# Linear attention and SwiGLU on one core: batch 0 in two halves of its heads, and the order of the first loads

## The chip, the cores and the metric

One core of a Trainium2 chip runs the whole program. The metric is the device time of one execution in microseconds (us); smaller is better. Executions of one kernel agree within about 0.4%. All runs quoted are of the state that the measurement calls fast. A ratio is the mean time of one kernel's fast runs over the mean of the other's fast runs of the same rounds, so it is not quite the ratio of the medians that stand beside it. The chip changed between the first measurement and the experiments, and between the three rounds of experiments (e1 to e4; e5 to e8; the last four). So each experiment is compared with the kernel before of its own round, and experiments of different rounds by their ratios.

PE is the matrix engine, ACT the scalar engine, DVE the vector engine, POOL the engine that issues the loads. PSUM is the memory that PE writes its results to, in banks. The granted clock is the share of its full speed that PE was given, as the profile records it.

## The reference, cut to what matters

```python
# q, k, v: (8 batches, 8 heads, 576, 64), float32
phi = lambda x: np.where(x > 0, x, np.exp(x) - 1.0) + 1.0     # = max(x, 0) + min(exp(x), 1)
kv  = einsum('bhsd,bhse->bhde', phi(k), v)                    # "kv", R in the kernel
z   = sum(phi(k), axis=2)
x   = einsum('bhsd,bhde->bhse', phi(q), kv) / (einsum('bhsd,bhd->bhs', phi(q), z) + 1e-6)
x   = x.transpose(0, 2, 1, 3).reshape(4608, 512)
out = (silu(x @ w_gate) * (x @ w_val)) @ w_out                # 512 -> 1536 -> 512
```

The kernel cuts the 4608 rows of x into nine groups of 512. A group has a first layer "L1" (12 blocks `fb`, each 8 matmuls for gate and value, then silu on ACT and a product on DVE) and a second layer "L2" (4 output tiles `t`, 12 matmuls each). A matmul of 128x512 starts 0.216 us after the one before it, so an L1 block is 1.73 us of PE and four L2 matmuls, a "piece", are 0.86 us. Group g of the feed-forward part overlaps with the attention of batch g+1. Groups 0 and 1 are special: nothing has been loaded yet, so loads, exps and layers start together.

Of the kernel before, what the change touches and what calls it, by code (L numbers as in the profile page):

```python
# [13 lines left out]
P = 128  # L14
# [3 lines left out]
def kernel(  # L18
# [78 lines left out]

    def load_0(src, dst):
        for lp in range(2):
            nc.gpsimd.dma_start(out=dst[0][:, 2 * lp:2 * lp + 2, :], in_=heads(src, 0)[:, 2 * lp:2 * lp + 2, :])  # L100

    def ld_k(b):
        load(k, k16, b)
# [50 lines left out]

    def terms_k(b):

        return (kp[1], kp[0]) if b == 0 else (kp[b % 2],)

    def mm1(b, lp):
        if lp == 0:  # L160
            kvb[b] = (bank(), bank()) if b != 1 else (pX[2], pV[2])
        W = 2 * D + (b > 1)
        for j in range(J):
            for term in terms_k(b):
                for hh in range(2):
                    rows = slice(C * hh, C * hh + C)
                    if b < 2:
                        vv = v16[b][rows, 2 * lp:2 * lp + 2, D * j:D * j + D]
                    else:
                        vv = vm[b % 2][rows, j, :, :].rearrange("p l c -> p (l c)")[:, 130 * lp:130 * lp + W]  # L170
                    nc.tensor.matmul(  # L171
                        out=kvb[b][hh][:, 256 * lp:256 * lp + W], lhsT=term[rows, j, P * lp:P * lp + P], rhs=vv,
                        start=(j == 0 and term is terms_k(b)[0]), stop=(j == J - 1 and term is terms_k(b)[-1]))

# [92 lines left out]
    def l1_banks(g, fb):  # L267
        if g > 0:
            return pG[(fb + 1) % 2], pV[(fb + 1) % 3]
        i = (fb + (fb > 5)) % 4  # L270
        return (pG[0], pG[1], pX[0], pX[1])[i], (pV[0], pV[1], pV[2], pX[2])[i]
# [12 lines left out]
    def l1(g, fb):  # L284
        for w in range(2):
            for i in range(4):
                l1_mm(g, fb, w, i)
        if (g, fb) == (0, 5):
            z0(1, 0)
            z0(1, 1)  # L290
            z0_copy(1)
        l1_gate(g, fb)
# [4 lines left out]
    def l2(g, t, f0=0, f1=FB):  # L297
        pso[(g, t)] = (pV[1], pG[1], pV[0], pG[0])[t]
        for fb in range(f0, f1):
            nc.tensor.matmul(out=pso[(g, t)][:, :], lhsT=hT[g % 2][:, fb, P * t:P * t + P], rhs=wo[:, fb, :],  # L300
                             start=(fb == 0), stop=(fb == FB - 1))
# [14 lines left out]
    def l2_last(g, t):  # L316

        banks = (pG[1], pX[0])
        for h in range(2):
            for fb in range(FB):  # L320
                nc.tensor.matmul(out=banks[h][:, 0:256], lhsT=hT[g % 2][:, fb, P * t:P * t + P],
                                 rhs=wo[:, fb, 256 * h:256 * h + 256], start=(fb == 0), stop=(fb == FB - 1))
        for h in range(2):
            o = osb[ot[0] % 4]
            ot[0] += 1
            for e in range(2):
                rows = slice(C * e, C * e + C)
                if e == 0:
                    nc.vector.tensor_scalar(out=o[rows, 0:256], in0=banks[h][rows, 0:256], scalar1=1.0 / SC,
                                            scalar2=None, op0=ALU.mult)  # L330
                else:
                    nc.scalar.activation(out=o[rows, 0:256], in_=banks[h][rows, 0:256], func=AF.Copy, bias=0.0,
                                         scale=1.0 / SC)
                b, j = units(g)[2 * t + e]
                (nc.sync, nc.scalar)[e].dma_start(
                    out=out[S * b:S * b + S, 256 * h:256 * h + 256].rearrange("(c j) f -> j c f", j=J)[j],
                    in_=o[rows, 0:256])


    load_0(k, k16)  # L340
    nc.gpsimd.iota(out=idx[:, :], pattern=[[-1, P]], base=0, channel_multiplier=1)
    load_0(q, q16)
    load_0(v, v16)
    ld_w1(0, 256)
    ld_k(1)
    ld_w1(256, 512)
    ld_q(1)
    ld_w1(512, 768)
    ld_w1(768, 1024)
    ld_w1(1024, 1280)  # L350
    ld_v(1)
    ld_w1(1280, 1536)
    ld_w2(0)


# [26 lines left out]
    def k_min(lp):  # L382
        term(ek, kp[0], lp, 1.0, ALU.min)

    def q_max(b, lp):
        term(q16[b], qp[1], lp, 0.0, ALU.max)
# [3 lines left out]

    zb0 = (pG, (pX[0], pV[2]))

    def z0(b, lp):
        ts = terms_k(b)
        for j in range(J):
# [6 lines left out]

    def z0_copy(b=0):
        for hh in range(2):
            nc.vector.tensor_scalar(out=zz[:, hh:4:2, :], in0=zb0[b][hh][:, 0:P].rearrange("p (l c) -> p l c", c=D),
                                    scalar1=1.0 / SC, scalar2=None, op0=ALU.mult)

# [13 lines left out]

    def r0_copies():
        for hh in range(2):
            kvv = kvb[0][hh][:, :].rearrange("p (i c) -> p i c", i=2)
            for h2 in range(2):
                rows, c = slice(D * h2, D * h2 + D), D * h2
                nc.vector.tensor_copy(out=R[0][rows, hh:4:2, :], in_=kvv[rows, :, c:c + D])

# [9 lines left out]

    warm(36, pX[1])
    for lp in range(2):  # L440
        exp0(k16[0], ek, lp)
        k_max(lp)
        k_min(lp)
    for lp in range(2):
        exp0(q16[0], eq, lp)
        q_max(0, lp)
        q_min(lp)
    z0(0, 0)
    warm(18, pX[1])
    z0(0, 1)  # L450
    z0_copy()
    warm(5, pX[1])
    t0(pV[0], 0, 0, 4)
    t0(pV[1], 0, 4, 8)
    t0_copy(pV[0], 0, 0, 4, A)
    t0_copy(pV[1], 0, 4, 8, A)
    warm(5, pX[1])
    t0(pV[2], 1, 0, 4)
    t0(pX[0], 1, 4, 8)
    t0_copy(pV[2], 1, 0, 4, V)  # L460
    t0_copy(pX[0], 1, 4, 8, V)
    turn[0] = 0
    mm1(0, 0)
    warm(1, pX[0])
    den0 = [pG[0][:, :], pG[1][:, :], pV[0][:, :], pV[1][:, :]]
    num0 = [pV[2][:, :], pX[0][:, :], pX[1][:, :], pX[2][:, :]]
    corners(den0, zz, 0, 0, 8)
    ln0(den0[0:2], rr[:, 0:2, :])
    exp_neg(rr[:, 0:2, :])
    for i in range(2, 4):  # L470
        ln0(den0[i:i + 1], rr[:, i:i + 1, :])
        exp_neg(rr[:, i:i + 1, :])
    mm1(0, 1)
    r0_copies()
    warm(8, pX[0])
    corners(num0, R[0], 0, 0, 8)
    for i in range(3):
        x0(num0[i], rr[:, i, :], xT[i][0][:, :])

# [6 lines left out]

    def phi_q1(lp):

        e = eq[:, 2 * lp:2 * lp + 2, :]
        nc.vector.tensor_scalar(out=e, in0=e, scalar1=1.0, scalar2=None, op0=ALU.min)  # L490
        d = qp[1][:, :, P * lp:P * lp + P].rearrange("p j (s d) -> p s j d", d=D)
        nc.vector.tensor_tensor(out=d, in0=d, in1=e.rearrange("p s (j d) -> p s j d", d=D), op=ALU.add)

# [38 lines left out]
    def r1_copies():  # L532
        for hh in range(2):
            kvv = kvb[1][hh][:, :].rearrange("p (i c) -> p i c", i=2)
            for h2 in range(2):
                rows, c = slice(D * h2, D * h2 + D), D * h2
                nc.vector.tensor_copy(out=R[1][rows, hh:4:2, :], in_=kvv[rows, :, c:c + D])

    def first():
        sl = at(FB, [  # L540
            (1, lambda: phi_k(1, 1)), (5, lambda: q_max(1, 0)), (5, lambda: q_max(1, 1)), (5, lambda: exp_q(1, 0)),
            (5, lambda: exp_q(1, 1)), (9, lambda: phi_q1(0)), (10, lambda: phi_q1(1)),
            (11, lambda: nc.scalar.preload_act_table_set("natural_log_exp_and_others"))])
        w = at(12, [
            (0, lambda: t1(pX[0], 0, 4, A)), (0, lambda: t1(pX[1], 4, 7, V)), (1, lambda: mm1(1, 0)),
            (1, lambda: mm1(1, 1)), (1, lambda: r1_copies()), (2, lambda: t1(pX[0], 7, 9, A)), (2, lambda: exp_k(2, 0)),
            (3, lambda: den1(0)), (3, lambda: phi_k(2, 0)), (4, lambda: num1(0)), (4, lambda: exp_k(2, 1)),
            (5, lambda: den1(1)), (5, lambda: phi_k(2, 1)), (6, lambda: num1(1)), (7, lambda: den2()),
            (8, lambda: num2()), (9, lambda: exp_q(2, 0)), (10, lambda: exp_q(2, 1))])
        return sl, w  # L550
# [27 lines left out]
    for i in range(4):  # L578
        for w in range(2):
            for fb in range(2):  # L580
                l1_mm(0, fb, w, i)
        if i == 0:
            for lp in range(2):
                t0(pV[2][:, P * lp:P * lp + P], lp, 8, 9)
            for lp in range(2):
                t0_copy(pV[2][:, P * lp:P * lp + P], lp, 8, 9, V)
            x0(num0[3], rr[:, 3, :], xT[3][0][:, :])
        if i == 1:
            d8 = [(pV[2], pX[0])[m % 2][:, part8[m]] for m in range(4)]
# [3 lines left out]
            exp_neg(r8[:, :, 0:P])  # L593
    ld_k(2)
    ld_w2(1)
    ld_w2(2)
    exp_k(1, 0)
    exp_k(1, 1)
    corners(n8, R[0], 0, 8, 9)
    for m in range(4):  # L600
        x0(n8[m], r8[:, m % 2, part8[m]], xT[m][1][:, 0:C])
    phi_k(1, 0)
    sl, w = first()
# [78 lines left out]
```

## The kernel before: the parts that the change and the argument touch

All loads go through one queue, in this order; the load casts float32 to fp16.

```python
    load_0(k, k16)                      # batch 0: k, q, v, each in two DMAs (heads 0-3, heads 4-7)
    load_0(q, q16)
    load_0(v, v16)
    ld_w1(0, 256);  ld_k(1)             # W1 (gate and value) in six column parts, batch 1 between them
    ld_w1(256, 512); ld_q(1)
    ld_w1(512, 768); ld_w1(768, 1024); ld_w1(1024, 1280)
    ld_v(1)
    ld_w1(1280, 1536)
    ld_w2(0)                            # W2 in three row parts
    # ... further down, after the first two L1 blocks:
    ld_k(2)
    ld_w2(1)
    ld_w2(2)
```

The list of what goes between the twelve L2 pieces of group 0 (the number is the piece after which it is placed). `den1`/`num1` are the denominators and numerators of batch 1, `exp_k(2, .)` the exps of batch 2's k, `t1(.., A)` transposes of batch 1's q with their copy on ACT, `mm1` the kv matmuls, `r1_copies` their copies from PSUM into R, `phi_k` the rest of phi on DVE, `den2` and `num2` the denominators and numerators of batch 1's last rows. ACT runs its instructions in this order.

```python
        w = at(12, [
            (0, lambda: t1(pX[0], 0, 4, A)), (0, lambda: t1(pX[1], 4, 7, V)), (1, lambda: mm1(1, 0)),
            (1, lambda: mm1(1, 1)), (1, lambda: r1_copies()), (2, lambda: t1(pX[0], 7, 9, A)), (2, lambda: exp_k(2, 0)),
            (3, lambda: den1(0)), (3, lambda: phi_k(2, 0)), (4, lambda: num1(0)), (4, lambda: exp_k(2, 1)),
            (5, lambda: den1(1)), (5, lambda: phi_k(2, 1)), (6, lambda: num1(1)), (7, lambda: den2()),
            (8, lambda: num2()), (9, lambda: exp_q(2, 0)), (10, lambda: exp_q(2, 1))])
```

The last output tile takes one buffer `osb` for both of its row halves, one written by DVE and one by ACT:

```python
        for h in range(2):
            o = osb[ot[0] % 4]
            ot[0] += 1
            for e in range(2):
                rows = slice(C * e, C * e + C)
                if e == 0:  nc.vector.tensor_scalar(out=o[rows, 0:256], in0=banks[h][rows, 0:256], ...)
                else:       nc.scalar.activation(out=o[rows, 0:256], in_=banks[h][rows, 0:256], ...)
                ...         # store by the SP queue (e == 0) or the ACT queue (e == 1)
```

## Time and profile before

| what | value | read from |
|---|---|---|
| time, median | 327.47 us (4 runs, 327.03 to 327.68) | timing |
| span of the profiled run | 324.9 us | page |
| PE busy | 98% | page, part 1 |
| first L1 matmul / first L2 matmul, group 0 | 18.85 / 42.00 us | timeline, PE |
| first L1 matmul, group 1 | 57.85 us | timeline, PE |
| k of batch 2 lands | 44.5 us | issue time plus time to landing |
| exp of k of batch 2 starts | 47.50 us | timeline, ACT |

The first lines are from the page of the kernel before: busy time by engine, then forty equal slices of the span (8.1 us each); a digit is the busy share in tenths, and the last row is what the DMA engines moved.

```profile
span 324.9 us, 5244 instructions
PE 318.3 (98%) x2033; PEld 152.1 (47%) x2033; DVE 215.0 (66%) x396; ACT 168.8 (52%) x251; POOL 31.7 (10%) x47
...
GB/s 105 197 203 197 204 208 207 244 193 79 115 137 121 68 93 143 99 70 92 162 79 94 81 98 2 24 74 95 11 26 51 95 34 0 27 91 12 0 33 98
```

PE is nearly full, so what can be won is idle time at the start. The GB/s row shows a second full resource: about 200 GB/s from the second slice to the seventh, without a gap. In that stretch a load lands when all loads ahead of it have landed. The tile view of k of batch 2 in the kernel before gives its issue (30.2 us) and the time to its landing:

```profile
L96 POOL DMA_DIRECT2D k_0_63<-in_k_dram x1: 740/740/740, 30.2 to 30.2; - x1
...
DMA to landing us min/median/max: 14.3/14.3/14.3
```

So it landed at 44.5 us. Doing this for every load gives 1.33 us for 256 KB, 2.55 us for 512 KB and 2.85 us for 576 KB, each after the one before it.

ACT has no idle time from the exp of k at 47.50 to the table load at 58.36, and k, landed at 44.5, was early.

### The profile page before, as it was taken

What the parts mean: (1) busy time and instruction counts of PE and PEld (TensorE: products, weight loads), DVE (VectorE), ACT (ScalarE), POOL (GpSimd) and SP (SyncE); (2) the same over time, 40 slices, a digit from 0 to 9 for tenths busy, and PEclk for the clock granted to TensorE, in tenths of its full rate; (3) what the DMA queues carried; (4) which work ended last, traced back from release to release, by engine and by line L of the source; (5) the groups of instructions that cost most, each with busy time, mean ns of one, the idle gap of its engine ahead of it and who ended that gap; (6) DMA issues with size and microseconds to landing.
All of it is one profiled execution on the core that took longest, in us unless ns stands there. A gap on an engine that the chain in (4) does not pass through costs nothing.

```text
span 324.9 us, 5244 instructions
## 1 busy us (share of the span) xinstructions
PE 318.3 (98%) x2033; PEld 152.1 (47%) x2033; DVE 215.0 (66%) x396; ACT 168.8 (52%) x251; POOL 31.7 (10%) x47
## 2 busy tenths in 40 slices
PE   8999999999999999999999999999999999999995
PEld 6844453444454445444444445444444444444443
DVE  2569559779967886798679857985797344243321
ACT  3687859657735674558456845584431233123310
POOL 8444400010001000100010000000000000000000
PEclk9999999999999999999999999999999999999999
DMA  7999999994577447634855340134012410140014
GB/s 105 197 203 197 204 208 207 244 193 79 115 137 121 68 93 143 99 70 92 162 79 94 81 98 2 24 74 95 11 26 51 95 34 0 27 91 12 0 33 98
DMA packets 40985, 32.20 MB, mean 99 GB/s; under 512 B 16256, under 2 KB 36480, under 8 KB 40960
## 3 DMA queue, kind: packets, MB, share of 16 engines
q0 software_dynamic: 20640, 18.88, 37.3%
q1 hardware_dynamic: 20160, 12.85, 17.5%
q8 instruction: 16, 0.26, 0.3%
q10 hardware_dynamic: 160, 0.13, 0.2%
q14 instruction: 9, 0.07, 0.1%
HBM read 37.75 MB, written 9.44 MB: 145 GB/s over the span
## 4 chain that ended last, share of the span: by engine, by line
PE 83%; DMA 7%; ACT 5%; DVE 2%; issue 1%; POOL 1%; POOLq 0%
PE pG_113 L275 13%; PE pG_112 L275 12%; PE pV_114 L275 9%; PE pV_115 L275 9%; PE pV_116 L275 8%; PE pV_114 L300 7%; PE pG_113 L300 7%; PE pV_115 L300 7%; PE pG_112 L300 6%; DMA wv<-in_moe_w_val_dram 4%; DMA v_0_67<-in_v_dram 3%; PE pX_117 L171 2%; PE pX_117 L247 1%; ACT rr L431 1%; ACT eq L122 1%
## 5 line engine op out<-in xcount | busy, mean ns | idle before, releaser
L275 PEld LDWEIGHTS <-wv 128*128 128x128 f16 x432 | 42.2, 98 | 51.5 <-DMA wv<-in_moe_w_val_dram 0.8
L275 PEld LDWEIGHTS <-wg 128*128 128x128 f16 x432 | 41.4, 98 | 51.3 <-issue 2.4
L280 ACT ACTIVATE sil_100<-pG_113 128x512 f16<-128x512 f32 x49 | 29.3, 597 | 49.8 <-PE pG_113 L275 49.0
L280 ACT ACTIVATE sil_101<-pG_112 128x512 f16<-128x512 f32 x50 | 29.8, 597 | 38.2 <-PE pG_112 L275 34.2
L300 PEld LDWEIGHTS <-hT_98 128*128 128x128 f16 x228 | 21.4, 98 | 25.6 <-issue 1.1
L300 PEld LDWEIGHTS <-hT_99 128*128 128x128 f16 x192 | 18.5, 98 | 22.7 <-issue 0.9
L310 DVE TENSOR_SCALAR osb_104<-pV_114 128x512 f32<-128x512 f32 x9 | 6.2, 690 | 17.2 <-PE pV_114 L300 17.2
L215 DVE TENSOR_REDUCE den<-prod 128x12 f32<-128x768 f16 x18 | 17.0, 943 | 0.0
L300 PE MATMUL pV_114<-wo,hT_98 128*128 128x512 f16 x60 | 14.1, 379 | 0.0
L300 PE MATMUL pG_113<-wo,hT_98 128*128 128x512 f16 x60 | 14.1, 379 | 0.0
L300 PE MATMUL pV_115<-wo,hT_98 128*128 128x512 f16 x60 | 14.1, 379 | 0.0
L308 ACT ACTIVATE osb_103<-pG_113 128x512 f32<-128x512 f32 x8 | 4.7, 584 | 16.3 <-PE pG_113 L300 16.3
L281 DVE SCALAR_TENSOR_TENSOR hT_98<-pV_115,sil_101 128x512 f16<-128x512 f32 x10 | 6.9, 690 | 8.1 <-ACT sil_101 L280 5.2
L310 DVE TENSOR_SCALAR osb_105<-pG_112 128x512 f32<-128x512 f32 x8 | 5.5, 692 | 9.7 <-PE pG_112 L300 9.7
L128 DVE SCALAR_TENSOR_TENSOR kp_72<-k_1_64,ek 128x576 f16<-128x576 f16 x16 | 11.4, 755 | 0.3
L300 PE MATMUL pG_112<-wo,hT_98 128*128 128x512 f16 x48 | 11.4, 380 | 0.0
L275 PE MATMUL pG_112<-xT_0_90,wg 128*128 128x512 f16 x28 | 10.6, 379 | 0.6 <-DVE xT_0_90 L437 0.3
L300 PE MATMUL pG_112<-wo,hT_99 128*128 128x512 f16 x48 | 11.1, 380 | 0.0
L300 PE MATMUL pV_115<-wo,hT_99 128*128 128x512 f16 x48 | 11.0, 379 | 0.0
L300 PE MATMUL pG_113<-wo,hT_99 128*128 128x512 f16 x48 | 11.0, 379 | 0.0
L300 PE MATMUL pV_114<-wo,hT_99 128*128 128x512 f16 x48 | 11.0, 379 | 0.0
L275 PE MATMUL pG_112<-xT_0_94,wg 128*128 128x512 f16 x28 | 10.6, 379 | 0.0
(245 smaller groups left out, 744.6 us busy)
## 6 DMA issues: line engine op xcount, KB each, us to landing
k_1_64<-in_k_dram POOLq DMA_DIRECT2D x4, 576.0 KB, 10.4
q_1_66<-in_q_dram POOLq DMA_DIRECT2D x4, 576.0 KB, 10.3
v_1_68<-in_v_dram POOLq DMA_DIRECT2D x4, 576.0 KB, 10.7
out_dram<-osb_102 SPq DMA_DIRECT2D x18, 128.0 KB, 2.4
out_dram<-osb_103 SPq DMA_DIRECT2D x18, 128.0 KB, 2.4
out_dram<-osb_104 SPq DMA_DIRECT2D x18, 128.0 KB, 2.4
out_dram<-osb_105 SPq DMA_DIRECT2D x16, 128.0 KB, 2.6
k_0_63<-in_k_dram POOLq DMA_DIRECT2D x3, 576.0 KB, 14.3
```

The costliest lines, as they stand in the source:

```text
L122: nc.scalar.activation(out=e[:, s, :], in_=src[b % 2][:, s, :], func=AF.Exp, bias=0.0, scale=1.0)
L128: nc.vector.scalar_tensor_tensor(out=dst[b % 2][:, :, D * l:D * l + D], in0=src[b % 2][:, l, :].rearrange("p (j d) -> p j d", d=D), scalar ...
L171: nc.tensor.matmul(out=kvb[b][hh][:, 256 * lp:256 * lp + W], lhsT=term[rows, j, P * lp:P * lp + P], rhs=vv, start=(j == 0 and term is term ...
L215: nc.vector.tensor_reduce(out=den[:, HL * j0:HL * j1], in_=prod[:, 0:j1 - j0, :].rearrange("p j (l d) -> p (j l) d", d=D), axis=AX.X, op=A ...
L247: nc.tensor.matmul(out=ps[2 * lp + e][C * hh:C * hh + C, :], lhsT=lhs[rows, 2 * lp + hh, :], rhs=qT[b % 2][rows, j0:j1, lp, C * hh:C * hh ...
L275: nc.tensor.matmul(out=ps[:, :], lhsT=src[:, i, P * fb:P * fb + P], rhs=xT[i][g % 2][:, :], start=(i == 0), stop=(i == 3))
L280: nc.scalar.activation(out=s[:, :], in_=pg[:, :], func=AF.Silu, bias=0.0, scale=1.0)
L281: nc.vector.scalar_tensor_tensor(out=hT[g % 2][:, fb, :], in0=pv[:, :], scalar=SC, in1=s[:, :], op0=ALU.mult, op1=ALU.mult)
L300: nc.tensor.matmul(out=pso[(g, t)][:, :], lhsT=hT[g % 2][:, fb, P * t:P * t + P], rhs=wo[:, fb, :], start=(fb == 0), stop=(fb == FB - 1))
L308: nc.scalar.activation(out=o[:, :], in_=ps[:, :], func=AF.Copy, bias=0.0, scale=1.0 / SC)
L310: nc.vector.tensor_scalar(out=o[:, :], in0=ps[:, :], scalar1=1.0 / SC, scalar2=None, op0=ALU.mult)
L431: nc.scalar.activation(out=dst[:, i, :], in_=src[i], func=AF.Ln, bias=epst[:, 0:1], scale=1.0)
```

## The change

The intent: PE's first L1 matmul waits for q.kv of all heads of batch 0. If heads 0 to 3 are taken through exp, z, denominators, kv and numerators first, L1 can start on their columns of x, while heads 4 to 7 follow between L1's passes. W1 is loaded earlier, since L1 will want it earlier, and k and q of batch 1 later. The diff, cut to its core:

```diff
-    load_0(k, k16)
+    load_0(k, k16, 0)
+    load_0(q, q16, 0)
     nc.gpsimd.iota(...)
-    load_0(q, q16)
-    load_0(v, v16)
+    load_0(q, q16, 1)
+    load_0(k, k16, 1)
+    for lp in range(2):
+        load_0(v, v16, lp)
     ld_w1(0, 256)
+    ld_w1(256, 512)
+    ld_w1(512, 768)
     ld_k(1)
-    ld_w1(256, 512)
-    ld_q(1)
-    ld_w1(512, 768)
     ld_w1(768, 1024)
     ld_w1(1024, 1280)
-    ld_v(1)
+    ld_q(1)
     ld_w1(1280, 1536)
     ld_w2(0)
+    ld_v(1)
 [cut: the prologue. exps, phi, z, den0(lp), num0(lp) now by half lp; num0(1) stands after L1's first pass]
-    ld_k(2)
-    ld_w2(1)
-    ld_w2(2)
-    exp_k(1, 0)
-    exp_k(1, 1)
 [cut]
+    ld_w2(1)
+    ld_w2(2)
+    ld_k(2)
 [cut: exps of batch 1's k and q in blocks after L1 blocks 3 and 7; z of batch 1 moved from L1 into L2]
-            (1, lambda: mm1(1, 1)), (1, lambda: r1_copies()), (2, lambda: t1(pX[0], 7, 9, A)), (2, lambda: exp_k(2, 0)),
-            (3, lambda: den1(0)), (3, lambda: phi_k(2, 0)), (4, lambda: num1(0)), (4, lambda: exp_k(2, 1)),
-            (5, lambda: den1(1)), (5, lambda: phi_k(2, 1)), (6, lambda: num1(1)), (7, lambda: den2()),
+            (2, lambda: mm1(1, 1)), (2, lambda: r1_copies()), (3, lambda: t1(pX[0], 7, 9, A)), (3, lambda: exp_k(2, 0)),
+            (4, lambda: den1(0)), (4, lambda: phi_k(2, 0)), (5, lambda: num1(0)), (5, lambda: exp_k(2, 1)),
+            (6, lambda: den1(1)), (6, lambda: phi_k(2, 1)), (7, lambda: num1(1)), (8, lambda: den2()),
-            (8, lambda: num2()), (9, lambda: exp_q(2, 0)), (10, lambda: exp_q(2, 1))])
+            (9, lambda: num2()), (9, lambda: exp_q(2, 0)), (10, lambda: exp_q(2, 1))])
 [cut: other PSUM banks for L1 and L2]
         for h in range(2):
-            o = osb[ot[0] % 4]
-            ot[0] += 1
             for e in range(2):
+                o = osb[ot[0] % 4]
+                ot[0] += 1
```

More of the change, by code (lines that the diff above doesn't have):

```diff
@@ L96, in load, with load_0 @@
         nc.gpsimd.dma_start(out=dst[b % 2][:, :, :], in_=heads(src, b))
-    def load_0(src, dst):
-        for lp in range(2):
-            nc.gpsimd.dma_start(out=dst[0][:, 2 * lp:2 * lp + 2, :], in_=heads(src, 0)[:, 2 * lp:2 * lp + 2, :])
+    def load_0(src, dst, lp):
+        nc.gpsimd.dma_start(out=dst[0][:, 2 * lp:2 * lp + 2, :], in_=heads(src, 0)[:, 2 * lp:2 * lp + 2, :])
     def ld_k(b):
@@ L153, with terms_k @@
     kvb = {}
-    def terms_k(b):
-        return (kp[1], kp[0]) if b == 0 else (kp[b % 2],)
+    def terms_k(b, lp):
+        return (kp[1], kp[0]) if (b, lp) == (0, 1) else (kp[b % 2],)
     def mm1(b, lp):
         if lp == 0:
-            kvb[b] = (bank(), bank()) if b != 1 else (pX[2], pV[2])
+            kvb[b] = (bank(), bank()) if b > 1 else ((pV[2], pX[0]), (pX[2], pV[2]))[b]
         W = 2 * D + (b > 1)
         for j in range(J):
-            for term in terms_k(b):
+            for term in terms_k(b, lp):
                 for hh in range(2):
@@ L172, in mm1 @@
                         out=kvb[b][hh][:, 256 * lp:256 * lp + W], lhsT=term[rows, j, P * lp:P * lp + P], rhs=vv,
-                        start=(j == 0 and term is terms_k(b)[0]), stop=(j == J - 1 and term is terms_k(b)[-1]))
+                        start=(j == 0 and term is terms_k(b, lp)[0]), stop=(j == J - 1 and term is terms_k(b, lp)[-1]))
     def zdiag(b, lp):
@@ L268, in l1_banks @@
         if g > 0:
-            return pG[(fb + 1) % 2], pV[(fb + 1) % 3]
-        i = (fb + (fb > 5)) % 4
+            return pG[fb % 2], pV[fb % 3]
+        i = fb % 4
         return (pG[0], pG[1], pX[0], pX[1])[i], (pV[0], pV[1], pV[2], pX[2])[i]
@@ L287, in l1 @@
                 l1_mm(g, fb, w, i)
-        if (g, fb) == (0, 5):
-            z0(1, 0)
-            z0(1, 1)
-            z0_copy(1)
         l1_gate(g, fb)
@@ L297, in l2 @@
     def l2(g, t, f0=0, f1=FB):
-        pso[(g, t)] = (pV[1], pG[1], pV[0], pG[0])[t]
+        pso[(g, t)] = (pV[0], pG[0], pV[1], pG[1])[t]
         for fb in range(f0, f1):
@@ L383, in k_min, with k_sum @@
         term(ek, kp[0], lp, 1.0, ALU.min)
+    def k_sum(lp):
+        c = slice(P * lp, P * lp + P)
+        nc.vector.tensor_tensor(out=kp[0][:, :, c], in0=kp[0][:, :, c], in1=kp[1][:, :, c], op=ALU.add)
     def q_max(b, lp):
@@ L389, in q_min @@
         term(eq, qp[0], lp, 1.0, ALU.min)
-    zb0 = (pG, (pX[0], pV[2]))
+    zb0 = (pG, (pX[2], pV[2]))
     def z0(b, lp):
-        ts = terms_k(b)
+        ts = terms_k(b, lp)
         for j in range(J):
@@ L401, in z0, with z0_copy @@
                                      stop=(j == J - 1 and t is ts[-1]))
-    def z0_copy(b=0):
+    def z0_copy(b, lp):
         for hh in range(2):
-            nc.vector.tensor_scalar(out=zz[:, hh:4:2, :], in0=zb0[b][hh][:, 0:P].rearrange("p (l c) -> p l c", c=D),
-                                    scalar1=1.0 / SC, scalar2=None, op0=ALU.mult)
+            nc.vector.tensor_scalar(out=zz[:, 2 * lp + hh, :], in0=zb0[b][hh][:, D * lp:D * lp + D], scalar1=1.0 / SC,
+                                    scalar2=None, op0=ALU.mult)
     def t0(dst, lp, j0, j1):
@@ L420, in t0_copy, with r0_copies @@
             nc.vector.tensor_copy(out=dst, in_=s3)
-    def r0_copies():
+    def r0_copies(lp):
         for hh in range(2):
-            kvv = kvb[0][hh][:, :].rearrange("p (i c) -> p i c", i=2)
-            for h2 in range(2):
-                rows, c = slice(D * h2, D * h2 + D), D * h2
-                nc.vector.tensor_copy(out=R[0][rows, hh:4:2, :], in_=kvv[rows, :, c:c + D])
+            for e in range(2):
+                rows, c = slice(D * e, D * e + D), 256 * lp + D * e
+                nc.vector.tensor_copy(out=R[0][rows, 2 * lp + hh, :], in_=kvb[0][hh][rows, c:c + D])
     def ln0(src, dst):
@@ L437, in x0, with den0, num0 @@
         nc.vector.scalar_tensor_tensor(out=dst, in0=src, scalar=1.0 / SC, in1=r, op0=ALU.mult, op1=ALU.mult)
-    warm(36, pX[1])
-    for lp in range(2):
-        exp0(k16[0], ek, lp)
-        k_max(lp)
-        k_min(lp)
-    for lp in range(2):
-        exp0(q16[0], eq, lp)
-        q_max(0, lp)
-        q_min(lp)
+    dbank0, nbank0 = (pX[1], pX[2]), ((pV[0], pV[1]), (pX[1], pX[2]))
+    def den0(lp):
+        corners({2 * lp + e: dbank0[e][:, :] for e in range(2)}, zz, 0, 0, 8, (lp,))
+        ln0([b[:, :] for b in dbank0], rr[:, 2 * lp:2 * lp + 2, :])
+        exp_neg(rr[:, 2 * lp:2 * lp + 2, :])
+    def num0(lp):
+        corners({2 * lp + e: nbank0[lp][e][:, :] for e in range(2)}, R[0], 0, 0, 8, (lp,))
+        for i in range(2 * lp, 2 * lp + 2):
+            x0(nbank0[lp][i % 2][:, :], rr[:, i, :], xT[i][0][:, :])
+    warm(42, pX[1])
+    exp0(k16[0], ek, 0)
+    exp0(q16[0], eq, 0)
+    exp0(q16[0], eq, 1)
+    k_max(0)
+    k_min(0)
+    k_sum(0)
+    q_max(0, 0)
+    q_min(0)
+    q_max(0, 1)
     z0(0, 0)
-    warm(18, pX[1])
-    z0(0, 1)
-    z0_copy()
-    warm(5, pX[1])
+    z0_copy(0, 0)
+    warm(4, pX[1])
     t0(pV[0], 0, 0, 4)
@@ L455 @@
     t0_copy(pV[0], 0, 0, 4, A)
-    t0_copy(pV[1], 0, 4, 8, A)
+    t0_copy(pV[1], 0, 4, 8, V)
+    exp0(k16[0], ek, 1)
     warm(5, pX[1])
-    t0(pV[2], 1, 0, 4)
-    t0(pX[0], 1, 4, 8)
-    t0_copy(pV[2], 1, 0, 4, V)
-    t0_copy(pX[0], 1, 4, 8, V)
-    turn[0] = 0
-    mm1(0, 0)
-    warm(1, pX[0])
-    den0 = [pG[0][:, :], pG[1][:, :], pV[0][:, :], pV[1][:, :]]
-    num0 = [pV[2][:, :], pX[0][:, :], pX[1][:, :], pX[2][:, :]]
-    corners(den0, zz, 0, 0, 8)
-    ln0(den0[0:2], rr[:, 0:2, :])
-    exp_neg(rr[:, 0:2, :])
-    for i in range(2, 4):
-        ln0(den0[i:i + 1], rr[:, i:i + 1, :])
-        exp_neg(rr[:, i:i + 1, :])
-    mm1(0, 1)
-    r0_copies()
-    warm(8, pX[0])
-    corners(num0, R[0], 0, 0, 8)
-    for i in range(3):
-        x0(num0[i], rr[:, i, :], xT[i][0][:, :])
+    den0(0)
+    q_min(1)
+    t0(pV[0], 1, 0, 4)
+    t0(pV[1], 1, 4, 8)
+    k_max(1)
+    k_min(1)
+    t0_copy(pV[0], 1, 0, 4, V)
+    t0_copy(pV[1], 1, 4, 8, V)
+    warm(3, pG[0])
+    z0(0, 1)
+    z0_copy(0, 1)
+    mm1(0, 0)
+    r0_copies(0)
+    den0(1)
+    warm(2, pG[0])
+    num0(0)
+    mm1(0, 1)
+    r0_copies(1)
     def at(n, items):
@@ L485, in at, with phi_1 @@
         return sl
-    def phi_q1(lp):
-        e = eq[:, 2 * lp:2 * lp + 2, :]
-        nc.vector.tensor_scalar(out=e, in0=e, scalar1=1.0, scalar2=None, op0=ALU.min)
-        d = qp[1][:, :, P * lp:P * lp + P].rearrange("p j (s d) -> p s j d", d=D)
-        nc.vector.tensor_tensor(out=d, in0=d, in1=e.rearrange("p s (j d) -> p s j d", d=D), op=ALU.add)
+    def phi_1(src, e, dst, lp):
+        s = slice(2 * lp, 2 * lp + 2)
+        nc.vector.tensor_scalar(out=e[:, s, :], in0=e[:, s, :], scalar1=1.0, scalar2=None, op0=ALU.min)
+        d = dst[1][:, :, P * lp:P * lp + P].rearrange("p j (s d) -> p s j d", d=D)
+        nc.vector.tensor_tensor(out=d, in0=d, in1=e[:, s, :].rearrange("p s (j d) -> p s j d", d=D), op=ALU.add)
     def t1(ps, j0, j1, eng):
@@ L537, in r1_copies, with block @@
                 nc.vector.tensor_copy(out=R[1][rows, hh:4:2, :], in_=kvv[rows, :, c:c + D])
+    def block(src, e, dst):
+        for lp in range(2):
+            exp_(src, e, 1, lp)
+            term(src[1], dst[1], lp, 0.0, ALU.max)
+        for lp in range(2):
+            phi_1(src, e, dst, lp)
     def first():
         sl = at(FB, [
-            (1, lambda: phi_k(1, 1)), (5, lambda: q_max(1, 0)), (5, lambda: q_max(1, 1)), (5, lambda: exp_q(1, 0)),
-            (5, lambda: exp_q(1, 1)), (9, lambda: phi_q1(0)), (10, lambda: phi_q1(1)),
+            (3, lambda: block(k16, ek, kp)), (7, lambda: block(q16, eq, qp)),
             (11, lambda: nc.scalar.preload_act_table_set("natural_log_exp_and_others"))])
         w = at(12, [
-            (0, lambda: t1(pX[0], 0, 4, A)), (0, lambda: t1(pX[1], 4, 7, V)), (1, lambda: mm1(1, 0)),
-            (1, lambda: mm1(1, 1)), (1, lambda: r1_copies()), (2, lambda: t1(pX[0], 7, 9, A)), (2, lambda: exp_k(2, 0)),
-            (3, lambda: den1(0)), (3, lambda: phi_k(2, 0)), (4, lambda: num1(0)), (4, lambda: exp_k(2, 1)),
-            (5, lambda: den1(1)), (5, lambda: phi_k(2, 1)), (6, lambda: num1(1)), (7, lambda: den2()),
-            (8, lambda: num2()), (9, lambda: exp_q(2, 0)), (10, lambda: exp_q(2, 1))])
+            (0, lambda: t1(pX[0], 0, 4, A)), (1, lambda: t1(pX[1], 4, 7, V)), (1, lambda: z0(1, 0)),
+            (1, lambda: z0(1, 1)), (1, lambda: z0_copy(1, 0)), (1, lambda: z0_copy(1, 1)), (2, lambda: mm1(1, 0)),
+            (2, lambda: mm1(1, 1)), (2, lambda: r1_copies()), (3, lambda: t1(pX[0], 7, 9, A)), (3, lambda: exp_k(2, 0)),
+            (4, lambda: den1(0)), (4, lambda: phi_k(2, 0)), (5, lambda: num1(0)), (5, lambda: exp_k(2, 1)),
+            (6, lambda: den1(1)), (6, lambda: phi_k(2, 1)), (7, lambda: num1(1)), (8, lambda: den2()),
+            (9, lambda: num2()), (9, lambda: exp_q(2, 0)), (10, lambda: exp_q(2, 1))])
         return sl, w
@@ L582 @@
         if i == 0:
+            num0(1)
+        if i == 1:
             for lp in range(2):
@@ L586 @@
                 t0_copy(pV[2][:, P * lp:P * lp + P], lp, 8, 9, V)
-            x0(num0[3], rr[:, 3, :], xT[3][0][:, :])
-        if i == 1:
+        if i == 2:
             d8 = [(pV[2], pX[0])[m % 2][:, part8[m]] for m in range(4)]
@@ L593 @@
             exp_neg(r8[:, :, 0:P])
-    ld_k(2)
-    ld_w2(1)
-    ld_w2(2)
-    exp_k(1, 0)
-    exp_k(1, 1)
+    nc.scalar.preload_act_table_set("silu_and_others")
     corners(n8, R[0], 0, 8, 9)
@@ L601 @@
         x0(n8[m], r8[:, m % 2, part8[m]], xT[m][1][:, 0:C])
-    phi_k(1, 0)
+    ld_w2(1)
+    ld_w2(2)
+    ld_k(2)
     sl, w = first()
```

## The prediction

> **What bounds the kernel now.** The matrix engine (PE): busy 98% of the 324.9 us span; from the timeline, weight-stage matmuls start every 0.216 us, and the waits by engine show only 2.4 us of named PE waits. So a change in the first stage is worth what it moves the first L1 matmul of group 1 (57.85 us). A second resource is full there: DMA moves about 200 GB/s without a pause from 8 to 65 us (slices row). Issue times plus issue-to-landing times give the landings: 256 KB every 1.33 us, 576 KB every 2.85; v's second half 14.6, W1 chunk 3 at 26.95/28.2, v of batch 1 at 36.5, W2 parts 41.65, 47.05, 49.6, k of batch 2 at 44.5.
>
> **What the change gains first.**
> - First L1 matmul: 18.85 before. It waits for q.kv of all heads. With halves, heads 0-3 are done once v's first half is in (13.5), heads 4-7 between L1's passes. I estimate L1 starting near 17 and block fb=2 near 21.6 instead of 23.1: 1.5 us.
> - PE waits for W1 at 26.57 and 27.84 total 0.85 us; chunk 3 now lands near 22.5, so they go.
> - z of batch 1 (about 0.6 us of PE) moves from L1 into L2: zero sum.
> - Two extra table switches are paid by ACT (1.28 us each), and four PSUM banks hide them.
> L2 of group 0 should start near 39.0 instead of 42.0: 3 us early.
>
> **Where it is taken back.** k of batch 2 now goes behind W2 parts 2 and 3 in the same queue. The bytes ahead of and including it equal those through W2's last part before, so it lands near 49.5, not 44.5. ACT executes in order (the Trainium skill, "TensorE: Matmul & The Clock Gate", architectural detail: ACT is strict FIFO; this trace shows no ACT instruction overtaking). exp of k, batch 2, heads 0-3 stands in ACT's order before the ln of batch 1's denominators. It started at 47.50; now it waits until 49.5. From there ACT was busy without a gap to 58.4, and PE's last waits in this stage end with that chain: exp_k at 47.50, the x written by DVE at 54.96, the L2 piece after num2 at 55.25. Shifted 2.0 us, num2 ends near 57.3; it now stands one L2 piece later (0.86 us), so two pieces remain instead of three. L1 of group 1 starts near 59.05 instead of 57.85: 1.2 us later, despite the 3 us won. PE then waits before den of batch 1's second heads (about 2 us) and before the two num's.
>
> **Tail.** l2_last takes a new output buffer for each half. The order of DVE then ACT goes (0.4 us), but the last ACT write now reuses the buffer of t=2, whose stores were issued at 319.0 and 319.54 and landed 2.2 to 2.4 us later, 321.95; it started at 321.37. I expect +0.6 us.
>
> **Prediction.** 327.56 + 1.2 + 0.6 = about 329.3 us; range 327.2 to 330.9. Faster by over 2%: 0.02; within 2%: 0.95; slower: 0.03.
>
> **What shows it right or wrong.** Timeline: first L1 matmul near 17; no PE wait for wg or wv; L2 group 0 at 39; an ACT wait of 2 us or more for k, ended by DMA near 49.5; first L1 matmul of group 1 near 59; ACT's last write waiting for a store.
>
> **What would make it wrong.** If k of batch 2 lands before 47, the 3 us stay and the time is near 325.5. If PE idles enough early to lose its granted clock the early gain shrinks, but up to 2 us of that is hidden behind the k wait.

## More of the kernel before

PE's timeline of the kernel before:

```profile
18.85 0.38 PE L275 MATMUL pG_112<-xT_0_90,wg 128*128 128x512 f16 x1 [0.33 <-DVE xT_0_90 L437]
...
57.85 0.38 PE L275 MATMUL pG_113<-xT_1_91,wg 128*128 128x512 f16 x1
...
69.87 0.38 PE L275 MATMUL pG_113<-xT_1_91,wg 128*128 128x512 f16 x1
```

The matmul at 69.87 is L1 block 6 of group 1.

ACT's timeline of the kernel before, at the seam from group 0 to group 1 (start, duration, engine, line, operation, output and input, and in brackets the idle time before it and what ended that):

```profile
47.01 0.60 ACT L503 ACTIVATE qT_89<-pX_117 128x512 f16<-128x512 f16 x1 [2.48 <-PE pX_117 L499]
47.50 1.16 ACT L122 ACTIVATE ek<-k_0_63 128x1152 f16<-128x1152 f16 x1
48.56 0.63 ACT L431 ACTIVATE rr<-pX_117,epst 128x448 f32<-128x448 f32 x1
...
58.36 1.28 ACT L622 ACT_TABLE_LOAD   x1
59.65 0.60 ACT L280 ACTIVATE sil_100<-pG_113 128x512 f16<-128x512 f32 x1
...
68.08 0.56 ACT L186 ACTIVATE R_86<-pX_117 64x128 f16<-64x128 f32 x2 [2.15 <-DVE zd L177]
68.64 0.56 ACT L186 ACTIVATE R_86<-pX_118 64x128 f16<-64x128 f32 x2
69.22 0.60 ACT L280 ACTIVATE sil_100<-pG_113 128x512 f16<-128x512 f32 x1
```

The chain of waits of this run (each step is what the next one waited for) holds ACT and DVE, and no PE, from 47.01 to 69.83 us. Its two ends, as start, length and work:

```profile
46.75 0.24 PE pX_117 L499 x4
47.01 0.60 ACT qT_89 L503
...
69.22 0.61 ACT sil_100 L280
69.87 1.02 PE pG_113 L275 x4
```

## The result, and the profile after

The changed kernel took 330.19 us (median of 4 runs, 329.72 to 331.00) against 327.47 us (4 runs, 327.03 to 327.68): ratio 1.0087, 95% interval 1.0063 to 1.0112. It is 2.7 us slower. That lies inside the predicted range (327.2 to 330.9), 0.9 us above the predicted 329.3.

PE's timeline of the changed kernel, with the lines that answer to those of before, the first L2 matmul of group 0, and two waits:

```profile
17.89 0.39 PE L274 MATMUL pG_112<-xT_0_90,wg 128*128 128x512 f16 x1
...
40.37 1.02 PE L295 MATMUL pV_114<-wo,hT_98 128*128 128x512 f16 x4 [0.18 <-DVE hT_98 L280]
...
51.29 0.35 PE L246 MATMUL pX_117<-qT_89,zz 64*64 64x448 f16 x1 [0.92 <-ACT rr L432]
...
59.06 0.38 PE L274 MATMUL pG_112<-xT_1_91,wg 128*128 128x512 f16 x1
...
71.93 0.38 PE L274 MATMUL pG_112<-xT_1_91,wg 128*128 128x512 f16 x1 [0.90 <-ACT sil_100 L279]
```

L1 starts 0.96 us earlier and L2 1.63 us earlier (42.00 to 40.37); the waits for W1 are gone. Then all of it is lost, and more: group 1 starts 1.21 us later and its block 6 2.06 us later. The tile view of k of batch 2, and ACT's timeline, in the changed kernel:

```profile
L96 POOL DMA_DIRECT2D k_0_63<-in_k_dram x1: 742/742/742, 31.2 to 31.2; - x1
...
DMA to landing us min/median/max: 18.3/18.3/18.3
```

```profile
46.98 0.60 ACT L513 ACTIVATE qT_89<-pX_117 128x512 f16<-128x512 f16 x1 [3.04 <-PE pX_117 L509]
49.56 1.16 ACT L121 ACTIVATE ek<-k_0_63 128x1152 f16<-128x1152 f16 x1 [1.98 <-DMA k_0_63<-in_k_dram]
50.63 0.62 ACT L432 ACTIVATE rr<-pX_117,epst 128x448 f32<-128x448 f32 x1
...
60.41 1.28 ACT L638 ACT_TABLE_LOAD   x1
61.71 0.60 ACT L279 ACTIVATE sil_100<-pG_112 128x512 f16<-128x512 f32 x1
...
70.14 0.55 ACT L185 ACTIVATE R_86<-pX_118 64x128 f16<-64x128 f32 x2 [3.01 <-DVE zd L176]
70.70 0.56 ACT L185 ACTIVATE R_86<-pX_119 64x128 f16<-64x128 f32 x2
71.28 0.60 ACT L279 ACTIVATE sil_100<-pG_112 128x512 f16<-128x512 f32 x1
```

k lands at 49.5 (31.2 + 18.3) instead of 44.5, since two W2 parts now go ahead of it. ACT stands idle 1.98 us for it, and every later line is about 2.06 us later than its partner before: 47.50 to 49.56, 58.36 to 60.41, 59.65 to 61.71, 69.22 to 71.28. The distance from the exp of k to L1 block 6 of group 1 is 22.37 us in both kernels (69.87 − 47.50 and 71.93 − 49.56).

The rest is at the end. The last ACT write of both kernels, before first:

```profile
321.37 0.38 ACT L332 ACTIVATE osb_102<-pX_117 64x256 f32<-64x256 f32 x1 [0.88 <-DVE osb_102 L329]
```

```profile
324.05 0.38 ACT L327 ACTIVATE osb_104<-pX_117 64x256 f32<-64x256 f32 x1 [1.56 <-DMA out_dram<-osb_104]
```

Counted from the start of the last group of matmuls (319.40 and 321.46 us), it starts after 1.97 us before and after 2.59 us in the change: 0.62 us more, waiting for the store of the tile before it. 2.06 + 0.62 = 2.68 us, which is the difference of the two spans (327.6 − 324.9 = 2.7). Both profiles are of executions a little faster than the medians (326.75 and 329.72 us).

### The profile page after: what moved, and what is told of

Its sections match the earlier page's. It is cut to its first block, busy times and chain, and to the rows that moved or that the text cites. A ratio compares the mean times of both kernels' runs of the same rounds, so it can differ in the third digit from the quotient of the medians.

```text
span 327.6 us, 5144 instructions
## 1 busy us (share of the span) xinstructions
PE 317.6 (97%) x1980; PEld 150.6 (46%) x1980; DVE 216.4 (66%) x406; ACT 170.5 (52%) x251; POOL 31.6 (10%) x47
## 3 DMA queue, kind: packets, MB, share of 16 engines
q0 software_dynamic: 20640, 18.88, 37.0%
HBM read 37.75 MB, written 9.44 MB: 144 GB/s over the span
## 4 chain that ended last, share of the span: by engine, by line
PE 80%; DMA 8%; ACT 6%; DVE 3%; issue 2%; POOL 0%; SPq 0%; ACTq 0%; POOLq 0%
PE pG_112 L274 12%; PE pG_113 L274 12%; PE pV_114 L274 8%; PE pV_115 L274 8%; PE pV_116 L274 8%; PE pV_115 L295 6%; PE pG_112 L295 6%; PE pV_114 L295 6%; PE pG_113 L295 6%; DMA k_0_63<-in_k_dram 6%; DMA q_0_65<-in_q_dram 2%; PE pX_118 L170 2%; PE pX_118 L246 1%; DMA out_dram<-osb_104 1%; ACT ek L121 1%
## 5 line engine op out<-in xcount | busy, mean ns | idle before, releaser
L279 ACT ACTIVATE sil_100<-pG_112 128x512 f16<-128x512 f32 x51 | 30.5, 597 | 48.9 <-PE pG_112 L274 48.4
L279 ACT ACTIVATE sil_101<-pG_113 128x512 f16<-128x512 f32 x51 | 30.4, 596 | 36.9 <-PE pG_113 L274 35.2
L305 DVE TENSOR_SCALAR osb_104<-pV_115 128x512 f32<-128x512 f32 x9 | 6.2, 691 | 17.2 <-PE pV_115 L295 17.2
L280 DVE SCALAR_TENSOR_TENSOR hT_98<-pV_114,sil_100 128x512 f16<-128x512 f32 x11 | 7.6, 688 | 7.7 <-PE pV_114 L274 5.5
L305 DVE TENSOR_SCALAR osb_105<-pG_113 128x512 f32<-128x512 f32 x8 | 5.5, 691 | 9.7 <-PE pG_113 L295 9.7
L280 DVE SCALAR_TENSOR_TENSOR hT_98<-pV_114,sil_101 128x512 f16<-128x512 f32 x8 | 5.5, 692 | 8.1 <-ACT sil_101 L279 5.2
L274 PE MATMUL pG_112<-xT_0_90,wg 128*128 128x512 f16 x27 | 10.3, 380 | 0.0
L305 DVE TENSOR_SCALAR osb_102<-pV_114 128x512 f32<-128x512 f32 x9 | 6.2, 690 | 6.1 <-PE pV_114 L295 6.1
```

The costliest lines, as they stand in the source:

```text
L274: nc.tensor.matmul(out=ps[:, :], lhsT=src[:, i, P * fb:P * fb + P], rhs=xT[i][g % 2][:, :], start=(i == 0), stop=(i == 3))
L279: nc.scalar.activation(out=s[:, :], in_=pg[:, :], func=AF.Silu, bias=0.0, scale=1.0)
L280: nc.vector.scalar_tensor_tensor(out=hT[g % 2][:, fb, :], in0=pv[:, :], scalar=SC, in1=s[:, :], op0=ALU.mult, op1=ALU.mult)
L305: nc.vector.tensor_scalar(out=o[:, :], in0=ps[:, :], scalar1=1.0 / SC, scalar2=None, op0=ALU.mult)
```

## The experiments

My theory: the late load of k (2.06 us) and the buffer of the last tile (0.62 us) are the loss. Rival A: the loss comes from batch 1's k and q, which are now loaded and exponentiated in two late blocks with two extra table switches. Rival B, from my own prediction: if k is on time, the early gain stays. Twelve kernels ran, all with correct results.

### e1: k of batch 2 back in front of W2

```diff
-    ld_w2(1)
-    ld_w2(2)
-    ld_k(2)
+    ld_k(2)
+    ld_w2(1)
+    ld_w2(2)
```

> The changed kernel with one line moved: the load of k of batch 2 is issued before W2 parts 2 and 3 again, as in the kernel before. My theory (k of batch 2 late at the scalar engine, 49.56 us, and from there 22.37 us of ACT and DVE work without a gap up to the L1 matmul of group 1 at 71.93): k lands near 44.5, exp of k starts when the copy of q's last transposes is out of the way (that copy was at 46.98), so at 47.5, and that L1 matmul starts at 69.9 as in the kernel before: span 325.5, time about 328.1, which is 2.1 below the change and still 0.6 above the kernel before (tail). The 1.6 us won before L2 of group 0 do not show, because the copy itself stands one L2 piece later. Rival A (the loss is from the later, blockwise k and q of batch 1 and its two extra table loads): no change, 330.2. Rival B (what my prediction said if k lands early: the early gain stays): near 325.5 to 326.

Measured: 327.60 us against 326.97, ratio 1.0022 (1.0002 to 1.0042). ACT's exp in e1 (names carry no numbers in the experiments' traces):

```profile
47.22 1.15 ACT L121 ACTIVATE ek<-k 128x1152 f16<-128x1152 f16 x1
```

k landed at 44.2 us, the exp followed the copy at 46.72 without a wait, and block 6 stood at 69.58, 22.36 us behind it. So 0.6 us remain of the 2.7, as my theory said. Rival A falls as the cause of the 2.1 us: batch 1's blocks are still late in e1. Rival B falls too: 325.5 was not reached. With k on time, the copy of q's last transposes, which the change put one L2 piece later, holds the chain at the old place. L1 of group 1 did start early (56.71 against 57.85 before); its block 6, where PE waited 0.90 us for a silu, hardly did (69.58 against 69.87).

### e2: the kernel before, with only that load moved back

```diff
-    ld_k(2)
     ld_w2(1)
     ld_w2(2)
+    ld_k(2)
```

> The kernel before with only that load moved behind W2 parts 2 and 3. My theory: k of batch 2 lands near 49.6 instead of 44.5, exp of k waits for it (47.5 before), the L1 matmul of group 1 that stood at 69.87 starts at 71.9, time 327.5 + 2.1 = 329.6. Rival A: about 327.5, since nothing of the halves is in it.

Measured: 328.52 us against 326.97, ratio 1.0056 (1.0041 to 1.0071): 1.55 us slower. k landed at 49.8, the exp started at 49.76 after a wait of 1.63 us for it, and block 6 at 72.14, again 22.38 us later. The single line makes the old kernel slow. It costs 0.5 us less than I expected. In this trace the copy was at 47.54, 0.5 us later than in the profile I had worked from, so less of the wait was new. Whether that is the reason is not shown: the kernel before was not profiled in this round, and block 6 of this run stands 2.27 us later than in the first profile (69.87).

### e3 and e4: the buffers of the last tile

e3 takes the old buffers back into the change; e4 gives the four pieces buffers of their own:

```diff
 e3:         for h in range(2):
+            o = osb[ot[0] % 4]
+            ot[0] += 1
             for e in range(2):
-                o = osb[ot[0] % 4]
-                ot[0] += 1
 e4:         for h in range(2):
             for e in range(2):
-                o = osb[ot[0] % 4]
-                ot[0] += 1
+                o = olast[2 * h + e]
 [cut: olast, four new buffers]
```

> The changed kernel with the output buffers of the last L2 tile as in the kernel before (one buffer for both engines' halves). My theory of the tail: the last ACT write no longer waits for the store of the tile before it (it started 2.59 us after the last matmul group's start in the change, 1.97 before): 0.6 us less, 329.6. Rival: the tail is not on the end of the time, or the serial order DVE then ACT costs as much: no change, 330.2.

> The changed kernel with four output buffers of their own for the last L2 tile: no order of DVE and ACT and no reuse of a buffer whose store is under way. My theory: the last ACT write starts with the last DVE write, 0.4 us before the kernel before's and 1.0 us before the change's, relative to the last matmul: time about 329.2.

Measured: e3 329.70 us, ratio 1.0088; e4 330.15 us, ratio 1.0098, both against 326.97. The times missed what I expected (329.2 for e4), and they cannot be compared with the change directly, which did not run on that chip in that round. The traces show the tail: from the start of the last matmul group to the last ACT write it is 1.96 us in e3 and 1.97 in e4, against 2.59 in the change. So the reuse costs 0.62 us in the trace. The times that bear on it are those of e1 and e11 (below), which differ in the tail alone: ratios 1.0022 and 0.9997, that is 0.8 us, on two chips. But the further 0.4 us that I expected of e4 do not exist. Its last ACT write:

```profile
324.36 0.38 ACT L327 ACTIVATE olast<-pX 64x256 f32<-64x256 f32 x1 [0.93 <-DVE olast L324]
```

It still starts 0.46 us behind DVE's write at 323.90, with no output buffer in common. What the two instructions still share is the PSUM bank that they read; a kernel with two banks was not tried, so that cause stays open.

The traces also pointed to why e3 and e4 were slow: block 6 stood 22.65 and 23.04 us behind the exp, not 22.37, and the granted clock of the run was 0.995. That gave a new theory, tested below.

### e5 to e8: is the ACT chain the bound once k is on time?

e5 is e1 with both exps of k of batch 2 placed before the copy that holds them; e6 is e1 with the copies of R of batch 2 three slots later, so that the silu of block 4 does not stand behind them; e7 is both, and the old tail; e8 is the kernel before with the two edits.

```diff
 e5: +  (2, lambda: exp_k(2, 0)), (2, lambda: exp_k(2, 1)), (3, lambda: t1(pX[0], 7, 9, A)),
     -  (3, lambda: t1(pX[0], 7, 9, A)), (3, lambda: exp_k(2, 0)),   ...   (5, lambda: exp_k(2, 1)),
 e6: -  (2, lambda: r_copies(b)),
     +  (2 + 3 * late, lambda: r_copies(b)),        # late is 1 for batch 2
```

> e1 (halves, k of batch 2 loaded before W2 parts 2 and 3) with both exps of k of batch 2 put before the copy of q's last transposes in ACT's order, where ACT stood idle for 3.0 us. My theory (in e1 the early gain is lost because ACT's chain of 22.4 us hangs on that copy at 46.7): 2.1 us of exp leave the chain, but ACT then waits for the den matmuls, so I expect silu of group 1 to start near 58.4 instead of 59.36 and the time about 1.0 below e1: 0.3 below the kernel before. Rival (the chain is not what bounds, the matrix engine's own work is): same as e1, 0.6 above before.

> e1 with the copies of R of batch 2 on ACT three slots later, so that the silu of L1 block 4 of group 1 isn't held behind them. In e1 L1 block 6 of group 1 waited 0.9 us for that silu. My theory: that wait goes, block 6 follows the zb matmul (68.31 + 0.2) instead of 69.58, time about 1.0 below e1, 0.4 below before. Rival: the next wait takes it back (zd on DVE is as late): within 0.2 of e1.

> e5 and e6 together, and the old buffers of the last tile (0.6 us, shown by e3 against the change). If both waits are in one chain and add up: block 6 of group 1 at about 67.6, time about 2.2 below before (0.993). If they overlap: about 1.6 below.

> The kernel before with the same two edits (exps of k of batch 2 before the copy of q's last transposes; R copies later), without the halves. My estimate: block 6 of group 1 at about 68.8 instead of 69.87, time 1.0 below before. The distance from this to e7 is what the halves are worth once ACT lets them through: my theory says about 1.2 us, of the 1.6 us by which L2 of group 0 starts earlier; a rival theory (the halves are worth nothing) says none.

Measured against 327.00 us: e5 327.84 (ratio 1.0023), e6 326.59 (0.9989), e7 326.00 (0.9975, 0.9962 to 0.9987), e8 326.13 (0.9978, 0.9966 to 0.9991).

In e6 the wait for the silu went, as I expected: block 6 started at 69.04, 0.21 us after the matmul before it, and by the ratios the time is 1.1 us below e1's. Block 6 came 0.54 us earlier than in e1 and not the 1.1 us that I expected, since PE now waited 1.14 us for W2's second part. e5 failed: it was no faster than e1. Its PE waited 1.15 us for W2's second part and 1.04 us for the silu behind the copies of R, and block 6 stood at 70.32, later than e1's 69.58. e7 gave 1.0 us and not the 2.2 or 1.6 that I had offered. The waits of PE in e7 (who waited for whom: total, times, longest) show what took it back:

```profile
PE pV L295 <- DMA wo<-in_moe_w_out_dram: 1.6, 1, 1.6
```

With k ahead of it, W2's second part lands at 47.4 us, and PE, 1.6 us early, waits for it. It is the same queue: whatever goes first, the other is late. That also bears on the question of e8: with k first, e7 and e8 differ by 0.1 us (326.00 against 326.13), which is inside the noise, and not by the 1.2 us of my theory. The rival theory of e8, that the halves are worth nothing, holds for this order of loads as far as these runs can tell.

### a1, e11 and e10: both causes undone, and the clock

a1 is the change again, on the chip of this round. e11 is the change with k first and the old tail (the edits of e1 and e3). e10 is the change with twelve filler matmuls before the numerators of batch 1, in front of PE's wait for k:

```diff
 e10: -  (5, lambda: num1(0)),
      +  (5, lambda: warm(12, nbank[0])), (5, lambda: num1(0)),
```

> The change as it stands, on the chip of the next three, for their comparison: 2.7 us above before, as recorded. Where PE's wait before the den matmuls of batch 1's second heads is near 2 us rather than 1, I expect the granted clock to fall under 1 after it (0.995 in three of its four timed runs, and in e3 and e4, where the wait was 1.9 us and the L1 matmul of group 1 that ends the ACT chain stood 22.65 and 23.04 us behind exp of k instead of 22.37).

> The change with both suspected causes undone: k of batch 2 before W2 parts 2 and 3, and the old buffers of the last tile. If the two are the whole loss and add up (2.1 + 0.6 of 2.7): equal to the kernel before within 0.3 us. If something else costs too: above it.

> The change with 12 filler matmuls (about 1.3 us of PE) before the num matmuls of batch 1's first heads, just before the wait for k that PE has there; their results are overwritten. Theory of the clock: the idle stretch takes the granted clock down, which adds 0.3 to 0.7 us to the 2.1 of the late k; with the filler the clock reads 1.0 in every run and the time is 0.3 to 0.6 below the change on the same chip. Rival: the clock has no part, filler work is at best free: same or higher.

Measured against 326.82 us: a1 330.63 (ratio 1.0122, 1.0102 to 1.0142), e11 326.83 (0.9997, 0.9983 to 1.0011), e10 329.79 (1.0095, 1.0078 to 1.0111).

e11: with the two causes undone, the change costs nothing and gains nothing. Its L2 of group 0 started at 38.95, and this is where about half of that lead ended:

```profile
47.01 1.02 PE L295 MATMUL pV<-wo,hT 128*128 128x512 f16 x4 [1.49 <-DMA wo<-in_moe_w_out_dram]
```

L1 of group 1 still started 1.0 us early (56.84 against 57.85 before). All but 0.16 us of that went in front of its block 6, where PE waited 0.91 us for a silu: 69.71 against 69.87.

a1 was 1.0122, not 1.0087: 3.8 us above before, where I expected 2.7. In its trace the early part went better: L2 of group 0 started at 39.46, against 40.37 in the first profile of the change, and PE then waited longer for k. The busy time of each engine in two stretches of a1 (the number after POOL's is the granted clock), then the second stretch in e10:

```profile
48.00:52.00 4.00, 2.06 (x13) 0.76 (x12) 1.29 (x3) 2.49 (x4) 0.00 (x0) 0.94 1.21 207
52.00:56.00 4.00, 4.00 (x24) 1.08 (x22) 3.76 (x7) 3.72 (x5) 0.00 (x0) 0.63 1.21 208
```

```profile
52.00:56.00 4.00, 3.53 (x26) 1.30 (x24) 3.75 (x8) 3.97 (x6) 0.00 (x0) 1.00 1.21 210
```

In a1, PE's longest wait was 1.76 us, and afterwards the granted clock was 0.63 on average over 4 us. Block 6 stood 22.81 us behind the exp of k. With the filler the longest wait was 1.05 us, the clock 1.00 in that stretch, and block 6 was 22.38 us behind the exp: 0.43 us less, though more work was done. The median is 0.84 us lower than a1's, more than the 0.3 to 0.6 that I expected; the intervals of the two ratios overlap, and the two profiled runs differ by 0.30 us only (330.06 and 329.76). So the traces show 0.3 to 0.4 us for the clock. The first measurement points the same way: the one run of the change at a clock of 1.0 took 329.72 us, the three at 0.995 took 329.89 to 331.00. The trace of a1, its fastest run, holds 3.0 us of loss (2.42 at block 6, 0.60 in the tail); what its other runs lost beyond that is in no trace. The expectation that the clock reads 1.0 in every run was a little too sharp: e10 shows 0.997 to 0.999, the kernel before 0.998 to 1.0, a1 0.995. The Trainium skill, "TensorE: Matmul & The Clock Gate", Part 1, says that the clock is halved after an idle window of about 3.4 us. Here it fell after a wait of 1.76 us already, so that figure does not fit.

### e9: a version that beats both

e7's trace pointed to the full queue as the limit. e9 is e7 with the order W2 part 2, k, W2 part 3; the exps of k behind the ln and exp of each half, so that nothing waits for k; and the copies of batch 2's v on POOL:

```diff
-    ld_k(2)
     ld_w2(1)
+    ld_k(2)
     ld_w2(2)
-  (2, lambda: exp_k(2, 0)), (2, lambda: exp_k(2, 1)), (3, lambda: t1(pX[0], 7, 9, A)), (4, lambda: den1(0)), ...
+  (3, lambda: t1(pX[0], 7, 9, A)), (4, lambda: den1(0)), (4, lambda: exp_k(2, 0)), (5, lambda: num1(0)), (5, lambda: phi_k(2, 0)),
+  (6, lambda: den1(1)), (7, lambda: num1(1)), (8, lambda: den2()), (8, lambda: exp_k(2, 1)), (9, lambda: num2()), ...
+    phi_k(2, 1)          # behind the last L2 piece of group 0
 in vcast:
+        if b == 2:
+            nc.gpsimd.tensor_copy(out=dst, in_=src)
 [cut: else the copy on ACT, as before]
```

> An attempt at a better kernel on e7. In e7, PE waited 1.6 us for W2 part 2, since k of batch 2 goes ahead of it and the queue is full. Here the order is W2 part 2, k, W2 part 3; the exps of k stand behind the ln and exp of each half, so ACT doesn't wait for k; and the two copies of v of batch 2 go to the POOL engine, which takes 2.3 us off ACT. My estimate: L1 of group 1 starts near 55.5 instead of 57.1, silu of group 1 at 58.8, block 6 of group 1 near 67.7 instead of 68.9: 1.0 to 1.3 below e7. If the copy on POOL takes over 3 us each, or if PE's own order is the bound, no gain. The theory under test: the full DMA queue, not ACT's work, holds e7.

Measured: 324.65 us against 326.82, ratio 0.9933 (0.9915 to 0.9951), 2.2 us below the kernel before and 6.0 us below a1. Two lines of e9, of ACT and POOL:

```profile
49.35 1.15 ACT L121 ACTIVATE ek<-k 128x1152 f16<-128x1152 f16 x1
```

```profile
55.41 2.26 POOL L150 COPY vm<-v 128x1152 f16<-128x1152 f16 x2 [19.46 <-DMA v<-in_v_dram]
```

k landed at 47.1, 2.2 us before its exp; PE's waits of 38 to 75 us add up to 0.5 us; L1 of group 1 started at 55.75 and block 6 stood at 67.56, near the 55.5 and 67.7 that I had expected. Here the early start of L2 (39.51 against 42.00 before) is still a lead of 2.3 us at block 6. By the ratios e9 is 1.4 us below e7. How much of that is the order and how much the copies on POOL was not separated, so the theory under test, that the queue and not ACT's work holds e7, is not decided. The kernel before was not tried with the same copies, so what the halves are worth here is not shown either.

## Why the prediction was right or wrong, point by point

- **Direction and place: right.** The prediction said that the gain before L2 is taken back by k of batch 2, late in a full queue, near 49.5 us. It landed at 49.5; e2 shows the same line slowing the old kernel, and e1 that putting it back removes 2.1 of the 2.7 us.
- **"First L1 near 17, L2 of group 0 near 39.0": too early in the profiled run** (17.89 and 40.37). It varies between runs: 38.95 to 40.37 in the traces of the change and of its variants e1, e3, e4, e10 and e11. As foreseen, it did not matter for the time, except by the clock: PE arrived later and waited 0.92 us for k, not the predicted 2.
- **"L1 of group 1 starts near 59.05": right** (59.06), **but the sum was mis-sized there.** I counted 1.2 us, taking PE's position at the start of group 1 as the end of the matter, and wrote nothing of what ACT and DVE still owed. The term is 2.06 us: the chain from the exp of k runs on through silu, phi of q, the diagonal of z and the copies of R to block 6 of group 1, 22.37 us in both kernels, and all of it moved. One L2 piece less after it does not shorten that chain. These 0.86 us are nearly all of the 0.9 us by which the forecast was too low. The chain of waits of the kernel before had shown ACT and DVE from 47.0 to 69.8 us; I read it for the first half only.
- **Tail: +0.6 us right (0.62), half of its reason wrong.** The wait for the store is as predicted. "The order of DVE then ACT goes (0.4 us)" fell: e4 keeps the order with buffers of its own.
- **Clock: named as a risk, and of the wrong sign.** I wrote that a lost clock would cost in the early part. It is lost later, after the wait for k, and in these traces where the early part was fast (L2 of group 0 at 39.46 to 39.62 in a1, e3 and e4, against 40.37): e10 puts it at 0.3 to 0.4 us in the traces, and at 0.84 us between the medians.
- **"If k lands before 47, the time is near 325.5": wrong.** e1 has k at 44.2 and takes 327.60; without the loss of the tail, e11 takes 326.83, level with the kernel before. The next limits lie close by: the copy of q's transposes with ACT's chain behind it (e1), and W2's second part (e7, e11).
- **Two extra table switches: right.** Each took 1.28 us, and no PE wait for silu shows in group 0.

## What to carry to other kernels

When a queue of loads is full, reordering it moves a wait rather than removing it: work out the landing time of every load that goes further back, and ask which in-order engine stands in front of it and what is behind that engine's next instruction. Follow the chain of waits to the point where the busiest engine takes over again, not only to the next stage boundary, and shift the whole chain. A lead at one point is worth something only if all that the next stage needs (here k, W2 and ACT's work) comes earlier too. In e9 the load order, the order on ACT and a third engine were changed together; which of them were needed was not tried.

## What the Trainium skill lacked or had wrong

- "TensorE: Matmul & The Clock Gate", HAM oscillation, asks for no PE gap over about 3.4 us. Here waits of 1.76 us (a1), 1.95 us (e3) and 1.94 us (e4) were followed by a granted clock of 0.57 to 0.64 over 4 us; waits of 1.49 us (e11) and 1.6 us (e7) were not. Where the limit lies was not measured.
- "ScalarE: Activation LUTs", What ACT_TABLE_LOAD costs, gives 1.28 us for the load and 1.38 us more for a drain. The trace agrees with 1.28 us, and shows no drain: in the change a silu follows its table load by 0.02 us (60.41 + 1.28 = 61.69, 61.71), the load starts 0.01 us after the end of the copy before it (60.40), and so the whole switch costs 1.3 us.
- No page has a rate for loads that cast. Casting loads of 256 to 576 KB, back to back in one queue, landed at 197 to 207 GB/s here (256 KB in 1.33 us, 576 KB in 2.85 us), counted as the fp16 that arrives; counted as the float32 that is read it is twice that (the page of the kernel before: 18.88 MB moved by this queue, 37.75 MB read from HBM). "DMA: Bandwidth & Descriptors", Bandwidth, has 341 GB/s for 1 MB in 6.15 us, but size over time is 170 GB/s, so it is not clear which bytes it counts, and the two are not compared here.
- "GPSIMD Engine Reference", 4.1 Engine selection, calls an operation with one input roughly line-rate on that engine, and gives no time. Here a copy of 128x1152 fp16 took 1.16 us on POOL (e9), and the same copy took 1.16 and 1.18 us on ACT in the kernel before (spans on POOL are rough).
